# Postmix with the seventh block of keys once per set of rows, and the last batch's rows written ahead of its ranking

## The chip, the cores and the metric

The kernel runs on one core of one Trainium2 chip. The metric is the time of one execution in microseconds of device time; less is better.

## The reference

Three layers in a row, in float32. Batch 4, 12 heads, 448 tokens of 64 values per head; then 1792 tokens of 768 values.

```python
scores = scale * np.matmul(q, k.transpose(0, 1, 3, 2))
scores = np.einsum('bhij,hg->bgij', scores, w_pre)       # premix of heads
attn = softmax(scores)                                   # rows divided by their sum + 1e-9
attn = np.einsum('bhij,hg->bgij', attn, w_post)          # postmix of heads
x = np.matmul(attn, v)                                   # then heads side by side: 1792 x 768
h = x @ w_in                                             # 768 -> 2048
x = elu(h) @ w_out                                       # 2048 -> 768
logits = x @ w_gate                                      # 8 experts, the best one is taken
for e in range(8):
    mask = argmax(logits) == e
    out[mask] = gate_w[mask, None] * (np.maximum(x[mask] @ w1[e], 0) @ w2[e])
```

## The kernel before, in words

One program of three stages, each with its own pools of tiles.

**Attention** (`attention`, to about 393 us). 448 queries of a batch are cut in four chunks (120, 120, 120 and 88 tokens), 16 chunks in all. The scores of a chunk (`qk`, L221, tile p_qk) are copied out and laid out again by DMAs (`relayout`, L238), so that 12 heads x T tokens (T is 5, in one set per batch 4) stand on 60 partitions; that is a row, and a set holds nr = 2 of them in each of two halves c of the 128 partitions. There are 92 sets: 88 with two rows and T = 5, 4 with one row and T = 4. Per set: `premix` (L247, p_pre) multiplies by the 60x64 matrix kpre; `rowmax` and `expo` (DVE, ACT) give pt, 128 x 2 x 448; `scale` (L268) makes kp, the postmix matrix of 60 columns with each row's reciprocal sum in it; `postmix` (L281, p_post) takes 64 keys of pt as weights and kp as moving operand, so that its result has the keys on the partitions; `mt_out` (L291, ACT) copies that to mt. `av` (L316, p_av) then multiplies mt by the values vt, 128 keys at a time, three times for each chunk.

448 keys are seven blocks of 64. The result of postmix has four columns of 128 keys, so the last has room for 128 where 64 are left: the loop makes eight products for seven blocks, the eighth (`k0 = min(s, 6)`) a repetition of the seventh, and `values` sets the upper 64 rows of the last block of values to zero with a GpSimd memset (L183). All operands are float32, and each matmul of the program stands in the trace as two records. Postmix uses 64x64 tiles of the array: the row half is c, the column half is s % 2.

The order of the work is made by a planner: `at(slot, order, fn)` files each step under a slot of the stage, and the steps run by slot and then by order. SP's queue issues the loads, POOL's the relayouts.

**The dense layer** (`moe1`, to about 880 us). The last batch is computed last: `omm(f)` adds up 16 slices of the output projection into acc (L579); in the last slice `evac(d)` copies each of six blocks of 128 outputs to x2, and `wide` (L604) and `logits` (L608, with L590) make the gate's logits for them. `route(b, x2)` returns the list of routing steps of a batch. For the last batch, ahead of the experts, nothing else is left to run beside them: `pick` (DVE, the expert of each token), `row(t, hf)` (three transposes of tile tp, L90, a copy by ACT, L639, and with hf = 1 the DMA of 112 tokens' rows to memory, L642, tile x2rows), `rank` (L689 to L728, the token's place with its expert), `ship` (the gates' DMA, L646), `sort` (L736, L738), `warm` (20 matmuls whose result nobody reads, L816), `order` (`places` makes sel, then the experts' order; SP reads it into registers, L776), `deal([first])` (tok1, the first expert's tokens, L786 and L790), and `before_end[2]`, which gathers that expert's rows (`gather`, xg, L1150). The first expert's weights w1raw are loaded at an address that hangs on the order (L1126).

**The experts** (`moe2`, to the end). `prep` splits a weight into a high and a low part (w1h by ACT, L110; w1l by DVE, L112), `trans` transposes the gathered rows (p_t, L90), `run` multiplies (p_h, L1203).

Of the kernel before, what the change touches and what calls it, by code (L numbers as in the profile page):

```python
# [5 lines left out]
F32 = mybir.dt.float32  # L6
# [4 lines left out]
ALU = mybir.AluOpType  # L11
# [136 lines left out]
S0 = [0]  # L148
# [6 lines left out]
def attention(tc, pools, at, q, k, v, kron_pre, kron_post, dec_jobs, xscr):  # L155
# [14 lines left out]
    kpo = sb.tile([128, 1, 60], F32, name="kpo")  # L170
    nc.gpsimd.dma_start(kpo[:, 0], kron_post)
    dec = Decoder(nc, early, DM // 2, 2, 2, 2)

# [6 lines left out]
    def values(b):  # L180
        vt[b] = sb.tile([128, 4, H, D], F32, name="vt", tag="vt", bufs=2)

        nc.gpsimd.memset(vt[b][S - 384:, 3], 0.0)  # L183

# [76 lines left out]
    def scale(cc, g):  # L261
        T, nr = UNITS[cc % 4][g]
        sm = sms.pop((cc, g))[:, :nr]
        nc.vector.tensor_scalar(sm, sm, 1e-9, None, ALU.add)
        nc.vector.reciprocal(sm, sm)
        kp = kpt[cc, g] = sb.tile([128, 2, 60], F32, name="kp", tag="kp", bufs=3)
        sh = [128, nr, 60]
        nc.vector.tensor_tensor(kp[:, :nr], kpo.to_broadcast(sh), sm.unsqueeze(2).to_broadcast(sh), ALU.mult)  # L268

    def postmix(cc, g):  # L270
        T, nr = UNITS[cc % 4][g]
        e, kp = pt.pop((cc, g)), kpt.pop((cc, g))
        p = pst[cc, g] = post_bank()
        for j in range(4):
            for r in range(nr):
                for s in range(2 * j, 2 * j + 2):

                    k0 = min(s, 6)
                    for c in range(2):
                        x = slice(64 * c, 64 * c + 12 * T)  # L280
                        mm(p[64 * (s % 2):64 * (s % 2) + 64, 2 * c + r, j * 12 * T:(j + 1) * 12 * T],  # L281
                           lhsT=e[x, r, 64 * k0:64 * k0 + 64],
                           rhs=kp[x, r].rearrange("p (h i) -> p h i", i=5)[:, :, :T], start=True, stop=True)

# [8 lines left out]
    def load_v(b, j):  # L293
        if j == 0 and b:
            values(b)
        n = min(128, S - 128 * j)
        nc.sync.dma_start(vt[b][:n, j], v[b, 128 * j:128 * j + n])

# [112 lines left out]
def moe1(tc, pools, at, w_in, w_out, w_gate, consts, xscr, wscr, oscr, x2rows, R, before_end):  # L411
    nc = tc.nc
    mm = nc.tensor.matmul
    P, x2 = {}, {}
    xs, xraw, rows32, wi, wo, hp, gs, es, op, acc, cst = ({} for _ in range(11))
    last_b = NB - 1

# [154 lines left out]
    def omm(f):  # L572
        (wh, wl), (gh, gl) = wo.pop(f), gs.pop((f, last_b))
        for d in range(KD):
# [5 lines left out]
            if f == NF - 1:  # L580
                evac(d)
                if d >= 2:
                    wide(d - 2)
        if f == NF - 1:
            lg = P["sb"].tile([128, DM], F32, name="lg", tag="dec_p", bufs=3)[:, :S]
# [7 lines left out]
    def evac(d):  # L593
        if d == 0:
            x2[last_b] = P["x2"].tile([128, KD, S], F32, name="x2", tag="x2", bufs=NG)
        if d % 2 == 0:
            nc.scalar.activation(x2[last_b][:, d, :], acc[d][:, :S], AF.Copy)
        else:
            nc.vector.tensor_copy(x2[last_b][:, d, :], acc[d][:, :S])
# [10 lines left out]

    def route(b, x2):

        sb, base = P["r"], cst["base"]
        sh = [JC, NJ, NE]
        last = b == NB - 1
        T, banks = {}, [0]

# [10 lines left out]
        def row(t, hf):  # L628
            if hf == 0 and last:
                if t % 2 == 0:  # L630
                    T["rows"] = P["sb"].tile([128, 2 * DM], F32, name="rows", tag="raw", bufs=2)[:JC]
                T["row"] = T["rows"][:, t % 2 * DM:(t % 2 + 1) * DM]
            elif hf == 0:
                T["row"] = P["sb"].tile([128, DM], F32, name="row", tag="dec_p", bufs=3)[:JC]
            p = bank([JC, 3, 128], "tp")
            for i in range(3):
                transpose(nc, p[:, i, :], x2[:, 3 * hf + i, t * JC:(t + 1) * JC], cst["ident"])
            dst = T["row"][:, hf * 384:(hf + 1) * 384].rearrange("p (a c) -> p a c", a=3)
            nc.scalar.activation(dst, p, AF.Copy)  # L639
            if hf == 1:  # L640
                r0 = 1 + b * S + t * JC
                nc.sync.dma_start(x2rows[r0:r0 + JC, :DM], T["row"])  # L642

# [126 lines left out]
        def order():  # L770
            places()
            gt, key = T["gt"], T["key"]
# [37 lines left out]
        if last:  # L810
            first = PLACES[0]

            def warm():
                p, t = bank([128, 512], "warm"), xs[b, 0][0]
                for i in range(20):
                    mm(p[:, :S], lhsT=t[:, :128], rhs=t, start=True, stop=True)  # L816

            def others():
                deal(range(NE))
                targets()  # L820

            return [pick, *rows[:2], rank, *rows[2:4], ship, *rows[4:], sort, warm, order,
                     lambda: deal([first]), before_end[2], others, keep, over]
        return [wide, rows[0], lambda: (narrow(), pick()), *rows[1:3], rank, *rows[3:6], sort,
# [123 lines left out]
    def rest():  # L948
# [20 lines left out]

        steps, banks, late = [], [0], []  # L970
        for n in range(3, NU + 1):
# [68 lines left out]
        for f in range(NF + 1):  # L1040
            if f < NF:
                hmm(f, last_b, h_bank)
                if steps:
                    steps.pop(0)()
                elu((f, last_b))
            if f >= 1:
                omm(f - 1)
                if f == NF:
                    assert not steps
                    steps += route(last_b, x2[last_b])  # L1050
                elif steps:
# [381 lines left out]
```

## Time and profile before

| | us, or a count |
|---|---|
| three runs | 1212.44, 1217.86, 1216.82 |
| their median | 1216.82 |
| the profiled execution | 1212.38 |
| its span in the trace | 1210.6 |
| PE busy | 1150.7 (95%) |
| DVE, ACT, POOL busy | 766.8, 684.0, 297.0 |
| PE instructions of the page | 13498, of them postmix 5760 |

The page is of one execution. Busy times are sums over instructions, a PE record's end is modelled, and matmuls on different 64x64 tiles of the array run at once, so the records of a line overlap. What a step costs is therefore read from the chain of waits, where each piece starts when the one before it lets go.

### The profile page before, as it was taken

How to read it: one execution, taken by the hardware profiler on the slowest of the kernel's cores; microseconds unless marked ns; L12 is line 12 of the kernel's file. 1: busy time of each engine (PE TensorE's matmuls, PEld its weight loads, DVE VectorE, ACT ScalarE, POOL GpSimd, SP SyncE). 2: the span in 40 equal slices, each digit the busy share in tenths (PEclk: the TensorE clock that was granted, in tenths of full speed). 3: DMA queues.
4: the chain of work that ended last, by engine and by line, in shares of the span. 5: the costliest groups of instructions: out<-in, count | busy, mean ns of one | idle time of the engine just before them, and what ended most of it. 6: DMA issues, size and time to landing. Idle time of an engine off the chain costs nothing.

```text
span 1210.6 us, 32469 instructions
## 1 busy us (share of the span) xinstructions
PE 1150.7 (95%) x13498; PEld 977.0 (81%) x13498; DVE 766.8 (63%) x1537; ACT 684.0 (57%) x1310; POOL 297.0 (25%) x470
## 2 busy tenths in 40 slices
PE   5899999989998999999999998999989999999995
PEld 1566656656676999999999987989779999999995
DVE  3766867766765778677776656545455555656662
ACT  2877877767866665555556344555434444555552
POOL 4755656646640003011121100000010110111110
PEclk8999999999998999999999999999979999999998
DMA  7687798886664436556482723334165755666651
GB/s 210 182 227 183 185 232 201 206 210 167 169 185 127 145 112 173 153 128 159 111 222 69 182 68 98 107 122 139 40 208 202 240 168 175 202 241 221 205 197 62
DMA packets 115617, 200.76 MB, mean 166 GB/s; under 512 B 44896, under 2 KB 75346, under 8 KB 115460
## 3 DMA queue, kind: packets, MB, share of 16 engines
q1 hardware_dynamic: 77284, 137.22, 36.2%
q0 software_dynamic: 38176, 61.37, 20.8%
q8 instruction: 108, 1.77, 0.7%
q14 instruction: 49, 0.40, 0.1%
HBM read 120.15 MB, written 30.09 MB: 124 GB/s over the span
## 4 chain that ended last, share of the span: by engine, by line
PE 87%; ACT 4%; DMA 3%; DVE 3%; issue 2%; POOL 0%; SPq 0%; POOLq 0%; ACTq 0%; DVEq 0%
PE p_h L513 14%; PE p_o L553 14%; PE p_h L1203 12%; PE p_z L1188 8%; PE p_post L281 7%; PE p_av L316 7%; PE p_pre L247 6%; PE p_qk L221 5%; PE acc L579 5%; PE p_o L513 4%; PE p_y L1203 3%; DMA sp<-st 2%; PE p_t L90 1%; ACT mt L291 1%; PE tp L90 1%
## 5 line engine op out<-in xcount | busy, mean ns | idle before, releaser
L238 POOL DMA_DIRECT2D sp<-st x360 | 207.5, 595 | 138.4 <-PE p_pre L247 69.4
L258 ACT ACTIVATE pt<-p_pre,mx 128x448 f32<-128x448 f32 x180 | 112.6, 632 | 48.1 <-DVE mx L252 47.9
L281 PEld LDWEIGHTS p_post<-kp,pt 60*64 60x64 f32 (+1 forms) x5760 | 96.4, 135 | 49.4 <-ACT mt L291 30.9
L291 ACT ACTIVATE mt<-p_post 128x960 f32<-128x960 f32 (+1 forms) x92 | 101.6, 1104 | 38.0 <-PE p_post L281 38.0
L281 PE MATMUL p_post<-kp,pt 60*64 60x60 f32 (+1 forms) x5760 | 108.2, 220 | 14.6 <-issue 9.9
L252 DVE TENSOR_REDUCE mx<-p_pre 128x1 f32<-128x448 f32 x180 | 104.1, 618 | 28.3 <-PE p_pre L247 22.1
L570 POOL DMA_DIRECT2D x<-part x46 | 41.5, 926 | 295.1 <-ACT part L569 289.4
L1203 PE MATMUL p_h<-xgh,w1h 128*128 128x256 f32 (+1 forms) x384 | 110.3, 287 | 0.2 <-DVE h2l L1206 0.2
L1203 PE MATMUL p_h<-xgl,w1h 128*128 128x256 f32 (+1 forms) x384 | 110.0, 286 | 0.2 <-DVE xgl L1167 0.2
L1203 PE MATMUL p_h<-xgh,w1l 128*128 128x256 f32 (+1 forms) x384 | 109.9, 286 | 0.0
L553 PE MATMUL p_o<-gh,woh 128*128 128x448 f32 x288 | 106.5, 370 | 2.6 <-DVE x L566 2.6
L221 PE MATMUL p_qk<-ks,qs 64*64 64x448 f32 x744 | 96.9, 552 | 12.7 <-issue 4.7
L247 PE MATMUL p_pre<-sp,kpre 60*64 60x448 f32 x720 | 100.9, 550 | 5.4 <-DMA sp<-st 5.4
L553 PE MATMUL p_o<-gl,woh 128*128 128x448 f32 x288 | 105.2, 365 | 0.0
L553 PE MATMUL p_o<-gh,wol 128*128 128x448 f32 x288 | 104.9, 364 | 0.0
L316 PEld LDWEIGHTS p_av<-mt,vt 128*64 128x64 f32 x1536 | 76.6, 141 | 32.9 <-DVE kp L268 9.9
L228 DVE COPY st<-p_qk 128x448 f32<-128x448 f32 x93 | 57.8, 622 | 71.5 <-PE p_qk L221 64.0
L112 DVE TENSOR_TENSOR w2l<-w2raw,w2h 128x768 fp32r<-128x768 f32 (+1 forms) x60 | 60.7, 1012 | 51.4 <-ACT w2h L110 51.4
L533 DVE SCALAR_TENSOR_TENSOR th<-rm,th 128x448 f32<-128x448 f32 x64 | 40.0, 625 | 80.0 <-ACT rm L532 80.0
L316 PE MATMUL p_av<-mt,vt 128*64 128x120 f32 (+1 forms) x1536 | 86.4, 268 | 1.4 <-issue 0.9
L1239 POOL DMA_INDIRECT out_dram<-yrow,put x18 | 23.8, 1321 | 254.2 <-ACT w1h L110 86.9
L112 DVE TENSOR_TENSOR w1l<-w1raw,w1h 128x768 fp32r<-128x768 f32 x64 | 61.0, 960 | 28.5 <-ACT w1h L110 26.4
(196 smaller groups left out, 2800.7 us busy)
## 6 DMA issues: line engine op xcount, KB each, us to landing
sp<-st POOLq DMA_DIRECT2D x352, 105.0 KB
w1raw<-in_w_dram SPq DMA_DIRECT2D x64, 384.0 KB, 6.9
w2raw<-in_w_dram SPq DMA_DIRECT2D x48, 384.0 KB, 3.4
x<-part POOLq DMA_DIRECT2D x46, 224.0 KB
raw<-in_w_in_dram SPq DMA_DIRECT2D x13, 768.0 KB, 4.1
raw<-in_w_out_dram SPq DMA_DIRECT2D x13, 768.0 KB, 7.6
wtmp<-wscr SPq DMA_DIRECT2D x19, 384.0 KB, 3.5
wtmp<-oscr SPq DMA_DIRECT2D x19, 384.0 KB, 4.1
```

The lines of the kernel that those rows point to most:

```text
L112: nc.vector.tensor_tensor(l, src, a.bitcast(F32), ALU.subtract)
L221: mm(p[e][64 * a:64 * a + 64, :S], lhsT=qq[r, c:c + 64], rhs=kk[r], start=True, stop=True)
L238: nc.gpsimd.dma_start(t[64 * r:64 * r + 12 * T, c], st[cc][f:f + d * (T - 1) + 1:d])
L247: mm(ban[r][64 * c:64 * c + 64, :S], lhsT=kpre[x], rhs=t[x, c, :], start=True, stop=True)
L252: nc.vector.tensor_reduce(mxs[cc, g][:, r:r + 1], pre[cc, g][r][:, :S], AX.X, ALU.min)
L258: nc.scalar.activation(pt[cc, g][:, r], pre[cc, g][r][:, :S], AF.Exp, bias=mxs[cc, g][:, r:r + 1], scale=-1.0, accum_out=sms[cc, g][:, r:r ...
L281: mm(p[64 * (s % 2):64 * (s % 2) + 64, 2 * c + r, j * 12 * T:(j + 1) * 12 * T], lhsT=e[x, r, 64 * k0:64 * k0 + 64], rhs=kp[x, r].rearrange ...
L291: nc.scalar.activation(dst, src, AF.Copy)
L316: mm(p[64 * e:64 * e + 64, u, :n], lhsT=vt[cc // 4][:, j, h, :], rhs=mt[cc][:, j * H + h, :n], start=(j == 0), stop=(j == 3))
L513: mm(p[:, :S], lhsT=a[:, c], rhs=m, start=(i == 0), stop=(i == 17))
L553: mm(p[:, :S], lhsT=a[:, c], rhs=m, start=(k == 0), stop=(k == 3 * len(fs) - 1))
L1203: mm(q[:, :N], lhsT=a[:, kk, :], rhs=m[:, kk, :], start=(j == 0), stop=(j == len(seq) - 1))
```

## The change

In `postmix` six blocks are multiplied as before, in another order of the loops. The seventh is multiplied once for each row: the product of row r goes to the column half h = r, and its moving operand is two of three neighbouring 60-column parts of kp, of which the middle one holds zeros: kp[0:2] for h = 0 and kp[1:3] for h = 1. So the upper half of the result's last column belongs to row 1 and the lower to row 0, with zeros for the other row, and the values of the last 64 keys are loaded twice, into both halves. kp becomes three fixed tiles. In `moe1`, four of the last batch's eight half rows run in the last slice of `omm`, after the fourth, fifth and sixth block; the other four run ahead of `rank`; each half row has its own DMA. `places` runs ahead of `ship` and `sort`; the first expert's tokens and its gather run ahead of `order`. `warm` has 24 matmuls.

```diff
+    kps = [sb.tile([128, 3, 60], F32, name=f"kp{i}") for i in range(3)]
+    for kp in kps:
+        nc.vector.memset(kp[:, 1], 0.0)
...
-        nc.gpsimd.memset(vt[b][S - 384:, 3], 0.0)
...
-        kp = kpt[cc, g] = sb.tile([128, 2, 60], F32, name="kp", tag="kp", bufs=3)
+        kp = kpt[cc, g] = kps[(S0[cc] + g) % 3]
...
-        nc.vector.tensor_tensor(kp[:, :nr], kpo.to_broadcast(sh), sm.unsqueeze(2).to_broadcast(sh), ALU.mult)
+        nc.vector.tensor_tensor(kp[:, ::2][:, :nr], kpo.to_broadcast(sh), sm.unsqueeze(2).to_broadcast(sh), ALU.mult)
...
-        for j in range(4):
+
+        def prod(s, r, c, out, w):
+            x = slice(64 * c, 64 * c + 12 * T)
+            mm(out, lhsT=e[x, r, 64 * s:64 * s + 64],
+               rhs=kp[x, w].rearrange("p w (h i) -> p w h i", i=5)[:, :, :, :T], start=True, stop=True)
+
+        for s in range(6):
             for r in range(nr):
-                for s in range(2 * j, 2 * j + 2):
-
-                    k0 = min(s, 6)
-                    for c in range(2):
-                        x = slice(64 * c, 64 * c + 12 * T)
-                        mm(p[64 * (s % 2):64 * (s % 2) + 64, 2 * c + r, j * 12 * T:(j + 1) * 12 * T],
-                           lhsT=e[x, r, 64 * k0:64 * k0 + 64],
-                           rhs=kp[x, r].rearrange("p (h i) -> p h i", i=5)[:, :, :T], start=True, stop=True)
+                for c in range(2):
+                    h, j = slice(64 * (s % 2), 64 * (s % 2) + 64), s // 2 * 12 * T
+                    prod(s, r, c, p[h, 2 * c + r:2 * c + r + 1, j:j + 12 * T], slice(2 * r, 2 * r + 1))
+        for h in range(2):
+            for c in range(2):
+                prod(6, min(h, nr - 1), c, p[64 * h:64 * h + 64, 2 * c:2 * c + nr, 36 * T:48 * T], slice(h, h + nr))
...
         n = min(128, S - 128 * j)
-        nc.sync.dma_start(vt[b][:n, j], v[b, 128 * j:128 * j + n])
+        for o in range(0, 128, n):
+            nc.sync.dma_start(vt[b][o:o + n, j], v[b, 128 * j:128 * j + n])
...
                 if d >= 2:
                     wide(d - 2)
+                if d >= 3:
+                    for fn in at_end[:2 if d == KD - 2 else 1]:
+                        fn()
+                        at_end.remove(fn)
...
-        T, banks = {}, [0]
+        T, banks = {}, [-1]
...
-            if hf == 1:
-                r0 = 1 + b * S + t * JC
-                nc.sync.dma_start(x2rows[r0:r0 + JC, :DM], T["row"])
+            r0, c0 = 1 + b * S + t * JC, hf * 384 if last else 0
+            if hf == 1 or last:
+                nc.sync.dma_start(x2rows[r0:r0 + JC, c0:(hf + 1) * 384], T["row"][:, c0:(hf + 1) * 384])
...
         def order():
-            places()
...
-                for i in range(20):
+                for i in range(24):
...
-            return [pick, *rows[:2], rank, *rows[2:4], ship, *rows[4:], sort, warm, order,
-                     lambda: deal([first]), before_end[2], others, keep, over]
+            at_end.extend(rows[::2])
+            rows = rows[1::2]
+            return [pick, *rows, rank, places, ship, sort, warm,
+                     lambda: deal([first]), before_end[2], order, others, keep, over]
```

The instructions of TensorE in the attention stage, a set's premix (p_pre), postmix (p_post) and the queries' products (p_qk) that follow. Before:

```order
L247 MATMUL p_pre_568<-sp_353,kpre_119 64x448
L247 MATMUL p_pre_569<-sp_353,kpre_119 64x448
L247 MATMUL p_pre_568<-sp_353,kpre_119 64x448
L247 MATMUL p_pre_569<-sp_353,kpre_119 64x448
L281 MATMUL p_post_588<-kp_576,pt_516 64x60 x32
L221 MATMUL p_qk_629<-ks_130,qs_290 64x448
L221 MATMUL p_qk_630<-ks_130,qs_290 64x448
```

Now, at a like place:

```order
L248 MATMUL p_pre_493<-sp_290,kpre_119 64x448
L248 MATMUL p_pre_494<-sp_290,kpre_119 64x448
L278 MATMUL p_post_512<-kp0_124,pt_441 64x60 x24
L278 MATMUL p_post_512<-kp0_124,pt_441 64x2x60 x4
L222 MATMUL p_qk_548<-ks_135,qs_295 64x448
L222 MATMUL p_qk_549<-ks_135,qs_295 64x448
```

32 products of 60 columns became 24 of 60 and 4 of twice 60; what stands around them stayed.

TensorE at the end of the dense layer: wide logits (p_h of 32 rows), the narrow ones (p_h of 112 x 8), the transposes of rows (tp of 112 x 128) and the ranking's products (rp). Before:

```order
L604 MATMUL p_h<-x_11745,wg 32x448
L608 MATMUL p_h<-wg,x_11745 112x8 x4
L590 MATMUL p_h<-sel,lg 112x8 x4
L608 MATMUL p_h<-wg,x_11745 112x8 x4
L90 MATMUL tp<-c_ident,x_11745 112x128 x6
L689 MATMUL rp<-base,c_ones 128x8
L690 MATMUL rp<-r_tot,c_tri 112x8
L691 MATMUL rp<-r_tot,c_ones 128x8
L90 MATMUL tp<-c_ident,x_11745 112x128 x18
L736 MATMUL tp<-tab,c_ident 128x24
```

Now:

```order
L615 MATMUL p_h<-x_11307,wg 32x448
L90 MATMUL tp<-c_ident,x_11307 112x128 x3
L619 MATMUL p_h<-wg,x_11307 112x8 x4
L601 MATMUL p_h<-sel,lg 112x8 x4
L619 MATMUL p_h<-wg,x_11307 112x8 x4
L90 MATMUL tp<-c_ident,x_11307 112x128 x12
L701 MATMUL rp<-base,c_ones 128x8
L702 MATMUL rp<-r_tot,c_tri 112x8
L703 MATMUL rp<-r_tot,c_ones 128x8
L748 MATMUL tp<-tab,c_ident 128x24
```

Three of the twelve early transposes show here, nine stand further ahead between the last slice's products; the other twelve are now in front of the ranking, where six were, and none is behind it.

VectorE at the end of routing: the places (r_pos, r_sel), the order of the experts, the first expert's tokens (tok_102) and all tokens (128 x 192). Before:

```order
L766 TENSOR_REDUCE r_pos<-r_gt 128x8
L768 SCALAR_TENSOR_TENSOR r_sel<-r_pos,c_em_6836 128x64
L773 TENSOR_TENSOR r_gt<-r_sel,c_em_6836 1x64
L774 TENSOR_REDUCE r_key<-r_gt 1x8
L775 TENSOR_SCALAR order<-r_key 1x8
L786 TENSOR_TENSOR pick<-tp,r_sel 128x24
L790 TENSOR_REDUCE tok_102<-pick 128x3
L786 TENSOR_TENSOR pick<-tp,r_sel 128x192
```

Now:

```order
L778 TENSOR_REDUCE r_pos<-r_gt 128x8
L780 SCALAR_TENSOR_TENSOR r_sel<-r_pos,c_em_6423 128x64
L797 TENSOR_TENSOR pick<-tp,r_sel 128x24
L801 TENSOR_REDUCE tok_102<-pick 128x3
L784 TENSOR_TENSOR r_gt<-r_sel,c_em_6423 1x64
L785 TENSOR_REDUCE r_key<-r_gt 1x8
L786 TENSOR_SCALAR order<-r_key 1x8
L797 TENSOR_TENSOR pick<-tp,r_sel 128x192
```

The three operations of the order moved behind the two that make the first expert's tokens. On SP's queue the last batch's transfers were two rows, the gates, two rows, and then the read of the order; they are now eight half rows, the gates, and the read of the order.

## Rows read from the trace of the kernel before

**Rows 1.** Part 1 of the page: engine, busy us, share, instructions.
```profile
PE 1150.7 (95%) x13498; PEld 977.0 (81%) x13498; DVE 766.8 (63%) x1537; ACT 684.0 (57%) x1310; POOL 297.0 (25%) x470
```

**Rows 2.** Part 4 of the page: shares of the chain by engine.
```profile
PE 87%; ACT 4%; DMA 3%; DVE 3%; issue 2%; POOL 0%; SPq 0%; POOLq 0%; ACTq 0%; DVEq 0%
```

**Rows 3.** Windows, attention: PE, PEld, DVE, ACT, POOL, clock, DMA share, GB/s.
```profile
20.00:380.00 360.00, 332.83 (x8650) 221.87 (x8651) 249.75 (x667) 263.72 (x566) 204.91 (x355) 0.99 0.74 191
```

**Rows 4.** Chain in order of time, attention: start, us, what, records.
```profile
199.68 0.45 PE p_post L281 x32
...
202.26 1.79 PE p_av L316 x32
...
206.65 1.36 PE p_av L316 x32
...
210.62 0.93 PE p_post L281 x64
```

**Rows 5.** Timeline of PE at the first postmix: start, us, what.
```profile
30.62 0.60 PE L247 MATMUL p_pre<-sp,kpre 60*64 60x448 f32 x3
30.99 0.26 PE L281 MATMUL p_post<-kp,pt 60*64 60x60 f32 x1
31.05 0.55 PE L247 MATMUL p_pre<-sp,kpre 60*64 60x448 f32 x3
```

**Rows 6.** Waits of PE, 24 to 380: total us, times, longest.
```profile
PE p_post L281 <- issue: 9.9, 11, 1.9
PE p_pre L247 <- DMA sp<-st: 5.4, 1, 5.4
PE p_qk L221 <- issue: 4.7, 3, 3.2
```

**Rows 7.** Part 3 of the page, instruction queue: packets, MB, share.
```profile
q8 instruction: 108, 1.77, 0.7%
```

**Rows 8.** Line 183: times, ns min/median/max, first and last start.
```profile
L183 POOL MEMSET vt<- x4: 732/777/787, 2.6 to 259.3; 64x768 f32 x4
```

**Rows 9.** Chain in order of time, at 839 and between the stages.
```profile
839.22 0.33 PE tp L90 x3
...
879.93 0.80 PE p_h L608 x8
...
882.13 0.54 PE rp L690 x2
...
883.10 3.93 PE tp L90 x18
...
887.58 3.30 DMA x2rows<-rows
...
891.76 1.06 POOL xg L1150
...
893.13 4.50 DMA xg<-x2rows,tok
...
897.67 1.54 PE p_t L90 x6
899.21 0.93 PE p_h L1203 x4
```

**Rows 10.** Timeline of ACT between the stages, idle time in brackets.
```profile
881.34 0.85 ACT L639 ACTIVATE rows<-tp 112x384 f32<-112x384 f32 x2
883.86 3.69 ACT L639 ACTIVATE rows<-tp 112x384 f32<-112x384 f32 x6 [1.67 <-PE tp L90]
```

**Rows 11.** Timeline of DVE between the stages.
```profile
887.63 0.18 DVE L790 TENSOR_REDUCE tok<-pick 128x3 uint32<-128x24 f32 x1
...
893.84 0.96 DVE L112 TENSOR_TENSOR w1l<-w1raw,w1h 128x768 fp32r<-128x768 f32 x1 [3.52 <-ACT w1h L110]
```

**Rows 12.** Timeline of SP between the stages.
```profile
889.21 10.01 SPq L1126 DMA_DIRECT2D w1raw<-in_w_dram  x7
```

**Rows 13.** Windows, the start of the experts; columns as in rows 3.
```profile
896.00:902.00 6.00, 5.72 (x26) 5.32 (x27) 2.93 (x7) 3.40 (x10) 1.26 (x2) 0.50 0.89 287
```

More of the change, by code (lines that the diff above doesn't have):

```diff
@@ L415, in moe1 @@
     xs, xraw, rows32, wi, wo, hp, gs, es, op, acc, cst = ({} for _ in range(11))
+    at_end = []
     last_b = NB - 1
@@ L594, in evac @@
         if d == 0:
-            x2[last_b] = P["x2"].tile([128, KD, S], F32, name="x2", tag="x2", bufs=NG)
+            x2[last_b] = P["x2_last"] = P["x2"].tile([128, KD, S], F32, name="x2", tag="x2", bufs=NG)
         if d % 2 == 0:
@@ L609, in logits, with route @@
                start=(d == KD - 2 and t == 0), stop=(d == KD - 1 and t == NJ - 1))
-    def route(b, x2):
+    def route(b, x2=None):
         sb, base = P["r"], cst["base"]
@@ L628, in row @@
         def row(t, hf):
[L629 to L632, printed above, removed]
+            if last:
+                if (t % 2, hf) == (0, 0):
+                    T["rows", t // 2] = P["sb"].tile([128, 2 * DM], F32, name="rows", tag="raw", bufs=2)[:JC]
+                T["row"] = T["rows", t // 2][:, t % 2 * DM:(t % 2 + 1) * DM]
             elif hf == 0:
@@ L635, in row @@
             p = bank([JC, 3, 128], "tp")
+            y = P["x2_last"] if last else x2
             for i in range(3):
-                transpose(nc, p[:, i, :], x2[:, 3 * hf + i, t * JC:(t + 1) * JC], cst["ident"])
+                transpose(nc, p[:, i, :], y[:, 3 * hf + i, t * JC:(t + 1) * JC], cst["ident"])
             dst = T["row"][:, hf * 384:(hf + 1) * 384].rearrange("p (a c) -> p a c", a=3)
             nc.scalar.activation(dst, p, AF.Copy)
-            if hf == 1:
-                r0 = 1 + b * S + t * JC
-                nc.sync.dma_start(x2rows[r0:r0 + JC, :DM], T["row"])
+            r0, c0 = 1 + b * S + t * JC, hf * 384 if last else 0
+            if hf == 1 or last:
+                nc.sync.dma_start(x2rows[r0:r0 + JC, c0:(hf + 1) * 384], T["row"][:, c0:(hf + 1) * 384])
         def ship():
@@ L968, in weights @@
             load_pair(f + 3)
-        steps, banks, late = [], [0], []
+        steps, banks, late, last_steps = [], [0], [], []
         for n in range(3, NU + 1):
@@ L1045, in rest @@
                 elu((f, last_b))
+            if f == NF:
+                last_steps += route(last_b)
             if f >= 1:
@@ L1049, in rest @@
                     assert not steps
-                    steps += route(last_b, x2[last_b])
+                    steps += last_steps
                 elif steps:
```

## The prediction

> **What bounds the kernel now.** I read the share of busy time first: TensorE is busy for 95% of the span [rows 1]. That is an average over three stages, so the chain of waits comes next: 87% of it is TensorE [rows 2]. The change touches two places. The first is the attention stage, from 20 to 380 us: there TensorE is busy 333 of 360 us, ScalarE 264, VectorE 250, GpSimd 205 [rows 3]. A time saved on TensorE shortens this stage, and no other engine is near to becoming its bound. The second is the step from the dense layer to the experts, between 880 and 899 us, where the chain leaves TensorE for VectorE, ScalarE and DMAs [rows 9].
>
> What does a postmix cost? Follow the pieces of the chain one by one [rows 4]. A set with 60 moving columns is 64 records in 0.93 us. They go to four 64x64 tiles of the array that work at once, so each tile makes 16 passes, and a round of four passes takes 0.93/16 = 58 ns. The set of 48 columns has 8 rounds in 0.45 us, 56 ns. A fifth fewer columns save 2 ns: at this width a pass is not set by its columns but by what comes with every pass, its weights. Value products (p_av) of 120 and 88 columns take 1.79/16 = 112 and 1.36/16 = 85 ns a round, so there 32 columns cost 27 ns, 0.84 ns each. By that slope 60 columns alone would be 50 ns, under the 58 measured, and a round of 120 columns about 50 more, 101; the p_av row itself says at most 112. I take 103.
>
> Do the tiles wait for each other? The timeline of the first postmix answers [rows 5]. One tile starts its postmix at 30.99; the other three tiles start their second premix passes only at about 31.05 and run them for 0.55 us. So a tile whose operands are there starts ahead of the others, and the order of the program counts only through how far it lies ahead in the queue.
>
> What the stage loses besides is in the waits [rows 6]: 9.9 + 4.7 = 14.6 us of "issue", when nothing visible holds TensorE up, and once 5.4 us for the first relayout. Instructions come from memory in packets, 108 in the whole run [rows 7].
>
> **Postmix, the product.** 88 of 92 sets have two sets of rows. Per set the change takes 8 products of 60 columns away (the seventh block, twice for each of two row sets and two column halves) and puts 4 of 120 columns in their place: 32 products become 28, the moving columns stay at 1920. Per tile 16 rounds of 58 ns become 12 of 58 and 2 of 103: 928 ns become 902, about -27 ns. The four sets of 48 columns keep their 16 products; zeros add columns to four of them, under 0.1 us each, which I cost at nothing.
>
> The order of the tiles changes too. Before, four products in a row go to four tiles; now two row sets follow each other on the same two tiles, and only then come the other two tiles. The second pair starts later by about one round, 58 ns; the bounds are nothing and two rounds, 117 ns. The query and premix products that follow start tile by tile, as in [rows 5], so the lag stays on its tiles and does not grow. It is paid where the next product needs both halves of the rows at once: that is p_av, three for each of 16 chunks, 48 in all. So 88 sets save 27 ns (-2.4 us) and 48 times a lag of 58 is paid (+2.8). I take **+0.4 us**; the bounds are -2.4 us (no lag) and 90 x 88 = +7.9 us (two rounds in every set).
>
> **Postmix, the instructions.** Each of the 88 sets loses 8 product records and 8 weight loads: 1408 of the stage's 17,301 [rows 3], 8.1%. If the issue stalls are instruction packets that come late, they shrink in proportion: 8.1% of 14.6 is **-1.2 us**. Between nothing and half of them (-7.3 us) I have no row that decides; it is the proportion that the count gives.
>
> **kp and the values.** VectorE writes the same 120 elements into every other column, and three fixed tiles are cleared at the start, while TensorE has no work; nothing. The GpSimd clearing of values goes: 4 x 0.78 us [rows 8] on an engine busy for 205 of 360 us, hidden before and worth nothing now. In its place 64 keys' values are loaded twice, four DMAs of 64 x 768 x 4 = 197 KB more on SP's queue: at 191 GB/s [rows 3] 1.0 us each. Three lie far from any need. The first, at the start, can push back the relayout for which TensorE waits 5.4 us; **+0.3 us**, between 0 and 1.0.
>
> **The step to the experts.** Call the end of the logits lp; before, 879.93 + 0.80 = 880.73 [rows 9]. Twelve transposes move ahead of it: at 0.33/3 = 0.11 us each, +1.32 us. ScalarE has the copy that follows one of them in front of the logits' own copy: 0.85/2 = 0.43 us [rows 10]. So lp comes 1.75 us later.
>
> Before, 18 transposes came after the ranking's products in 3.93 us, 0.218 each, twice the 0.11, and the last row transfer took 3.30 and landed at 890.88, lp + 10.15; the gather was built from 891.76 [rows 9]. Now 12 transposes in four pieces are left: the first piece 3 x 0.218 = 0.65, then four copies at 3.69/6 = 0.61 [rows 10], then 3.30: lp + 6.4. The gather also needs the tokens, at 887.63 + 0.18, lp + 7.08 [rows 11]. Three VectorE operations of the order (0.65 us with their gaps) and a wait of 0.26 for TensorE no longer stand in front: lp + 6.2. But the ranking's products now queue behind 12 transposes, lp + 1.3 at full clock, lp + 2.6 at half, where it was lp + 1.40 [rows 9]: up to 1.2 later, so lp + 6.2 to 7.4. The gather is free at lp + 6.4 to 7.4 in place of 10.15: -2.7 to -3.7 against +1.75. I take **-1.5 us** net.
>
> Two things are late next. The first expert's weight load cannot go before the order is read: it was issued at 889.21, lp + 8.48 [rows 12]; the order is now made behind the tokens, so about 0.4 to 0.6 later against lp. Its splitting ended at 893.84 + 0.96 [rows 11], 5.6 us after the issue, so now near lp + 14.6; the first product, at 899.21 before [rows 9], would start at lp + 18.5 - 3.2 = lp + 15.3: just hidden. It takes up to 1 us if the gather gains all. And the clock: TensorE goes from 896 to 902 at half its clock, 0.50, the 1.2 GHz level [rows 13], after TensorE had waited for the gather's 4.50 us [rows 9]. Four more warming products and a shorter gap may spare part of this; at most half of the 1.54 us of transposes and 0.93 of first products [rows 9], -1.2. I take nothing. Bounds of this step: -3.2 and +0.5. SP has eight row transfers instead of two pairs, each half as long and issued as soon as its copy is done; that is in the path above, and the gate's transfer stays last.
>
> **Sum.** 0.4 - 1.2 + 0.3 - 1.5 = -2.0 us against the profiled execution, 1212.4 us, so 1210.4. That execution is the fastest of four: the median of the runs is 1216.8 and the mean of all four 1214.9. Against that mean a new median would be **1212.9 us**. A difference under 0.5% (6.1 us) can hardly be told from none here, so "same" is 1210.7 to 1222.9.
>
> **Rivals.**
> *Fetching was the limit (0.20).* If the stalls come from a fetch that is only just too slow, 8% fewer instructions can take half of them: -7.3 instead of -1.2, 1206.8 us. For it: 14.6 us without a visible cause. Against it: they are 14 stalls of up to 3 us, not a steady shortfall.
>
> *Tiles in program order (0.09), the slower side.* If a product had to wait for the one before it, whichever its tile, the new order would make each pair a step of its own: two products of 117 ns on the same tiles before the other pair moves, 7 x 117 + 206 = 1025 ns per set and up to 58 more, against 928. Then +97 to +155 ns x 88 = +8.5 to +13.6, in the middle +11.1 instead of +0.4: 1223.6 us. It decides from about 118 ns per set on (118 x 88 = 10.4, which ends at 1222.9). Against it: one tile starts alone [rows 5]. The Trainium skill ("TensorE: Matmul & The Clock Gate", Part 3, "The mechanism") says that matmuls start and end strictly in the order of the program; by that rule this rival would hold. What hangs on it here is only whether a start at 30.99 ahead of one at 31.05 was in program order.
>
> *Loads and products take turns (0.03).* If, in a tile, a weight load could not run under the product before it, every load removed would save its full length: two passes fewer per tile, 2 x 58 = 116 ns x 88 = -10.2 us in place of +0.4, 1202.3 us. Against it: 16 passes of 58 + 50 = 108 ns would take 1.73 us and the row says 0.93 [rows 4]. The Trainium skill (same page and section) says that weight loads overlap running matmuls only when the row groups differ, which would be this case for passes of one tile; the measured 58 ns a round disagree.
>
> *The step gains nothing (0.08).* The ranking or the weight load takes the place of the rows: 1214.4 us.
>
> **Chances.** The forecast has 0.60; of it 0.10 falls under 1210.7 and 0.02 over 1222.9, since the runs shown spread over 5 us. Faster: 0.10 + 0.20 + 0.03 = 0.33. Slower: 0.09 + 0.02 = 0.11. Same: 0.56. The range, 1205.0 to 1221.5, takes in the fetch rival at its low end and, at its high end, the bound of two late rounds (1212.9 + 7.5 = 1220.4, and 1.1 of the other bounds); it leaves out the program-order and the take-turns rivals, 0.12, and the forecast's tails.
>
> **What would show it.** Postmix pieces of the chain near 0.90 us; 1.02 or more everywhere means program order. Issue waits of about 13.4 us in the stage. The row transfers landed and the gather issued about 2 us earlier, near 889 to 890, and the first expert product near 897.7. I am wrong if attention as a whole moves by more than 5 us either way.

## The result, and the profile after

The change ran at a median of 1203.55 us (1198.01 to 1206.79, six runs), the kernel before in the six runs beside it at 1215.95 (1212.44 to 1220.33): 12.4 us less. The ratio of the two is 0.9869 with an interval of 0.9837 to 0.9901; the quotient of these two medians, 0.9898, lies inside it. Forecast were 1212.9 us and a range of 1205.0 to 1221.5: the gain is real, larger than forecast, and ends under the range. The profiled execution took 1198.01 us, the fastest of its six; that of before, 1212.38 us, was faster than all six of before. They are 14.4 us apart.

Where the 14.4 us lie, by the starts and ends of TensorE's records in the two traces:

| stretch | before | change | difference |
|---|---|---|---|
| start to first postmix | 31.0 | 32.2 | +1.2 |
| first to last postmix | 347.7 | 336.2 | -11.5 |
| last postmix to the end of the last acc | 498.7 | 499.0 | +0.3 |
| end of the last acc to the first expert product | 21.5 | 18.1 | -3.4 |
| first expert product to the end | 311.7 | 310.7 | -1.0 |

Four fifths are in the attention stage. Part 1 of the page after, part 3's row of the instruction queue and part 4, to be held against [rows 1, 7, 2]:

```profile
PE 1148.1 (96%) x12798; PEld 975.4 (82%) x12798; DVE 766.2 (64%) x1540; ACT 683.5 (57%) x1310; POOL 295.4 (25%) x466
...
q8 instruction: 103, 1.69, 0.6%
...
PE 88%; ACT 4%; DVE 3%; DMA 2%; issue 1%; POOL 0%; SPq 0%; POOLq 0%; ACTq 0%; DVEq 0%
```

TensorE is busy 2.6 us less, the span is 14.4 us shorter: what went is mostly time in which TensorE stood still. 700 matmuls and five packets of instructions are gone. The waits of TensorE in the attention stage after, against [rows 6]; columns: total us, times, longest:

```profile
PE p_post L278 <- issue: 4.9, 6, 1.5
PE p_post L278 <- ACT mt L296: 4.8, 8, 1.2
PE p_qk L222 <- ACT st L231: 2.8, 3, 1.0
...
PE p_pre L248 <- DMA sp<-st: 1.1, 1, 1.1
```

The issue waits (idle time of TensorE that nothing visible ends), 9.9 + 4.7 + 0.9 (ahead of p_av) = 15.5 us before, are 4.9. That is 10.6 of the stage's 11.5 us. One more piece goes with the longest of these stalls before. Timeline and windows there (columns as in [rows 3]):

```profile
269.64 0.59 PE L221 MATMUL p_qk<-ks,qs 64*64 64x448 f32 x2 [3.20 <-issue]
...
270.90:274.30 3.40, 3.40 (x30) 2.65 (x29) 2.57 (x8) 1.34 (x4) 1.93 (x4) 0.50 0.41 132
```

After 3.2 us of standing still the granted clock was 0.50, the 1.2 GHz level, for 3.4 us. Between the first and the last postmix of the change it was 1.00 throughout. The step to the experts in the chain of waits after, against [rows 9]:

```profile
870.67 0.80 PE p_h L619 x8
...
877.55 0.18 DVE tok L801
...
878.68 1.07 POOL xg L1165
879.75 0.30 issue
880.05 4.54 DMA xg<-x2rows,tok
884.64 0.34 PE p_t L90
```

The logits end at 871.47, the tokens stand at 877.73, 6.3 us later, and the gather is built from 878.68, 7.2 us after them, where before it was built 11.0 us after the logits. The row transfers are gone from the chain: the tokens are now what the gather waits for. The clock there, windows of the same trace (columns as in [rows 13]):

```profile
877.00:880.00 3.00, 3.00 (x10) 2.69 (x9) 2.58 (x15) 0.00 (x0) 1.07 (x1) 0.50 0.00 0
880.00:884.00 4.00, 3.59 (x21) 3.04 (x19) 1.30 (x5) 0.85 (x1) 1.01 (x1) 1.00 0.86 292
884.60:890.60 6.00, 5.55 (x41) 4.94 (x42) 4.24 (x9) 3.84 (x12) 2.73 (x3) 1.00 0.94 338
```

The first six us of the experts, at 0.50 before, ran at 1.00; the fall to 0.50 now comes earlier, and the first warming products ran in it (877 to 880).

### The profile page after: what moved, and what is told of

The parts are those of the page before. It is cut to its first block, busy times and chain, and to the rows that moved or that the text cites. A ratio compares the mean times of both kernels' runs of the same rounds, so it can differ in the third digit from the quotient of the medians.

```text
span 1196.2 us, 31070 instructions
## 1 busy us (share of the span) xinstructions
PE 1148.1 (96%) x12798; PEld 975.4 (82%) x12798; DVE 766.2 (64%) x1540; ACT 683.5 (57%) x1310; POOL 295.4 (25%) x466
## 4 chain that ended last, share of the span: by engine, by line
PE 88%; ACT 4%; DVE 3%; DMA 2%; issue 1%; POOL 0%; SPq 0%; POOLq 0%; ACTq 0%; DVEq 0%
PE p_h L520 14%; PE p_o L560 14%; PE p_h L1218 11%; PE p_z L1203 8%; PE p_post L278 7%; PE p_av L322 7%; PE p_pre L248 6%; PE p_qk L222 5%; PE acc L586 5%; PE p_o L520 4%; PE p_y L1218 3%; DMA sp<-st 1%; ACT mt L296 1%; PE p_t L90 1%; PE tp L90 1%
## 5 line engine op out<-in xcount | busy, mean ns | idle before, releaser
L278 PEld LDWEIGHTS p_post<-kp,pt 60*64 60x64 f32 (+1 forms) x5056 | 88.6, 134 | 44.1 <-ACT mt L296 31.1
L278 PE MATMUL p_post<-kp,pt 60*64 60x60 f32 (+2 forms) x5056 | 108.9, 228 | 10.0 <-issue 4.9
L248 PE MATMUL p_pre<-sp,kpre 60*64 60x448 f32 x720 | 105.9, 551 | 3.8 <-DMA sp<-st 3.8
L222 PE MATMUL p_qk<-ks,qs 64*64 64x448 f32 x744 | 100.0, 557 | 9.0 <-ACT st L231 5.1
L112 DVE TENSOR_TENSOR w1l<-w1raw,w1h 128x768 fp32r<-128x768 f32 x64 | 60.9, 960 | 28.3 <-ACT w1h L110 25.1
```

What stands on the lines that cost most here:

```text
L112: nc.vector.tensor_tensor(l, src, a.bitcast(F32), ALU.subtract)
L222: mm(p[e][64 * a:64 * a + 64, :S], lhsT=qq[r, c:c + 64], rhs=kk[r], start=True, stop=True)
L248: mm(ban[r][64 * c:64 * c + 64, :S], lhsT=kpre[x], rhs=t[x, c, :], start=True, stop=True)
L278: mm(out, lhsT=e[x, r, 64 * s:64 * s + 64], rhs=kp[x, w].rearrange("p w (h i) -> p w h i", i=5)[:, :, :, :T], start=True, stop=True)
```

## The experiments

The question was what took the issue waits away, since the forecast had given them 1.2 us. The theory: they are instruction packets that land late (a packet lands when its transfer is complete). The rivals: shorter products, the number of instructions, the burst within a set. Time ratios are to the kernel before on the same chip.

**The step alone, and postmix alone.** The first has the attention of before in the change, the second the `moe1` of before.

```diff
 # e1: attention() of before, moe1() of the change
 # e8: attention() of the change, moe1() of before
```

> The change without its attention part: only the step to the experts is as in the change. Both theories of the attention gain (late instruction packets; shorter products) expect the same here: the attention stage as before, issue waits of TensorE between 20 and 380 us near 15.5 us, the last postmix near 378.7 us. The step itself should give back what the two traces differ by behind the last slice of the dense layer, -3.2 us: about -3 us against before, and the wait for the gather to end about 13.2 us after the logits instead of 16.9.

> The attention part of the change alone, with the old step to the experts. If the parts add up: the ratio to before that is left of the change's 0.987 without the step's 0.998 (2.8 us by the traces), 0.989, so 11 to 13 us under before; issue waits of 5 to 9 us. If the step carried more than the step-alone run could show: 8 us or less.

Measured: the step alone 0.9994 (0.9966 to 1.0023), issue waits 9.5 + 4.2 + 1.5 = 15.2 us. Postmix alone 0.9922 (0.9891 to 0.9953), 9.5 us less; its issue waits, forecast at 5 to 9 us, are 12.3 in the profiled execution, the slowest of its eleven (1215.78 us). So most of the gain is postmix's. The step is too small for the runs; in the traces, the stretch from the last postmix to the end takes 829.1 us on average (827.4 to 830.2) in nine executions of this study that have it (e16, with 828.4, not counted), and 831.1 (829.7 to 832.5) in the six that don't, 2.0 us less. 9.5 and 2.0 are 11.5, near the 12.4 of the medians (16.3 by e13's medians).

**30 products, 32 products, another order of tiles.**

```diff
 # e2, on before
+                    if s == 7 and r:
+                        continue
+                    n = nr if s == 7 else 1
...
-                        mm(p[64 * (s % 2):64 * (s % 2) + 64, 2 * c + r, j * 12 * T:(j + 1) * 12 * T],
+                        mm(p[64 * (s % 2):64 * (s % 2) + 64, 2 * c + r:2 * c + r + n, j * 12 * T:(j + 1) * 12 * T],
...
-                           rhs=kp[x, r].rearrange("p (h i) -> p h i", i=5)[:, :, :T], start=True, stop=True)
+                           rhs=kp[x, r:r + n].rearrange("p w (h i) -> p w h i", i=5)[:, :, :, :T], start=True, stop=True)
 # e3, on the change
-                prod(6, min(h, nr - 1), c, p[64 * h:64 * h + 64, 2 * c:2 * c + nr, 36 * T:48 * T], slice(h, h + nr))
+                for i in range(nr):
+                    prod(6, min(h, nr - 1), c, p[64 * h:64 * h + 64, 2 * c + i:2 * c + i + 1, 36 * T:48 * T],
+                         slice(h + i, h + i + 1))
 # e4, on the change
-        for s in range(6):
+        for s2 in range(3):
             for r in range(nr):
-                for c in range(2):
+                for s, c in ((2 * s2, 0), (2 * s2, 1), (2 * s2 + 1, 0), (2 * s2 + 1, 1)):
 # e7: e4 with e3's products, i as the outer loop
```

> The kernel before, in which the repeated eighth product is made once for each half of the rows, with 120 moving columns, instead of twice with 60 (what it gives is multiplied by the zeros in the values, as before). 30 products for a set instead of 32, half of the change's cut in instructions, and the tiles of the other column half keep their 16 passes, so that a set takes as long as before. If late instruction packets were the limit: issue waits well under 15.5 us, between 5 and 12, and the time 3 to 8 us under before. If the products had become shorter: nothing is gained, within 1 us of before, and the issue waits stay near 15 us.

> The change, with each of its four products of 120 columns cut into two of 60: 32 products for a set again, and all else as in the change. If late instruction packets were the limit: issue waits back at 13 to 17 us, while a set that nothing interrupts is at most 30 ns longer than in the change; the time 8 to 13 us over the change, about that of the step alone. If the weight loads that are saved were the gain, undisturbed sets become longer by 60 to 120 ns each and the issue waits stay near 5 us. If neither, the time is within 3 us of the change.

> The change, with its 24 products of 60 columns in the old order, in which four products in a row go to four tiles. By the prediction's lag of one round, paid at each of 48 value products, this gains 2.8 us and the pieces ahead of value products get shorter by some 58 ns; if the lag is not paid, the time is within 1 us of the change. If tiles in program order cost anything, it gains 8 us or more.

> The rotating version of the change with its four products of 120 columns cut into eight of 60 that go round the four tiles: 32 products, the order of before, the step to the experts as in the change. It differs from the rotating version by 4 products a set and nothing else. Late packets: issue waits at 14 to 16 us again, and 9 to 13 us over the change, about 1216; the undisturbed set as long as before. If the 14.8 us that the unpaired version lost were all due to its order of tiles: within 3 us of the change.

Measured: 30 products 0.9954 (0.9929 to 0.9979), issue waits 13.5 us, where 5 to 12 were expected; 32 products in the new order 1.0006 (0.9979 to 1.0033), 15.0 us; 28 products in the old order of tiles 0.9877 (0.9840 to 0.9913), 9.2 us; 32 products in the old order 1.0045 (1.0013 to 1.0076). The waits of the third, e4, and of the last, e7, which differ in the number of products alone:

```profile
PE p_post L278 <- issue: 7.1, 7, 2.2
...
PE p_qk L222 <- issue: 1.4, 1, 1.4
...
PE p_av L322 <- issue: 0.7, 1, 0.7
```

```profile
PE p_post L278 <- issue: 10.5, 13, 2.2
...
PE p_qk L222 <- issue: 4.2, 3, 2.9
...
PE p_av L324 <- issue: 1.6, 2, 1.2
```

Four products a set, 8% of the instructions, bring the issue waits back to 16 us. The order of the tiles is worth nothing (1204.86 against 1203.55 us): the lag of one round that the forecast charged at p_av is not paid. In the five traces with 32 products in one piece and all loads (before, e1, e3, e7, e11) the issue waits are 15.0 to 16.3 us; in the six with 28 (the change, e4, e8, e12, e13, e14) 4.9 to 12.3. The ranges do not overlap.

The rival of shorter products has a part. Take the sets without value products that nothing interrupts for over 100 ns, at full clock, from the first product of a set to that of the next. The median is 2491 ns in before, e1, e7 and e15 (32 products), 2478 in e2 (30) and 2464 in the change, e4, e8, e13 and e14 (28), over 35 to 45 sets in each. 27 ns for each of 88 sets are 2.4 us at most. With the 7.3 us by which the issue waits fell on average (below) that comes near e8's 9.5.

e7 is the slowest of these, 1224.13 us, though e1 with as many products is level with before. In the traces its attention stage is 5.9 us longer than e1's, 1.1 of it issue waits; in e7 the clock was at 0.50 for three stretches of 3.4 us between first and last postmix, in e1 for none.

**Burst within a set.** A set's products in two halves, with the query products between (e5 on before, e6 on the change), or with p_av between (e10 on before).

```diff
-            at(x + LAG + .5, 10, postmix, cc, g)
+            at(x + LAG + .5, 10, postmix, cc, g, 0)
+            at(x + LAG + 1, 9.5, postmix, cc, g, 1)
...
 # e10: slots x + LAG + .5 with orders 8.5 and 10
```

> The kernel before, with each set's 32 products in two halves of 16 and the next query products (8 records in 0.76 us) between them: as many instructions as before, but no more than 64 product records in a row. If the stalls come from the burst, that is, a packet is used up within a set faster than the next one comes: issue waits well under 15.5 us, 3 to 9, and 5 to 10 us less time. If they go by the number of instructions alone: issue waits stay at 14 to 16 us and the time within 2 us of before. The copy of a set to mt comes 0.8 us later; where TensorE waits for that copy, 4.6 us in all before, it may wait up to 4 us more.

> The change with its 28 products split in the same way, 16 and then 8 and 4 of 120 columns. If the burst makes the stalls: the 5 to 9 us of issue waits that the change and its rotating version still have fall under 3, and the time is 3 to 6 us under the change. If the number makes them: no change, within 2 us.

> The kernel before, with a set's 32 products in two halves of 16 around the value products (p_av) where a set has them: 48 of 92 sets have no more than 64 product records in a row, the order of all else and the waits for ScalarE stay. Two forms of the theory of late packets are told apart, since the split around the query products was mixed up with 21 us of new waits for ScalarE. If the burst within a set makes the stalls: issue waits fall from 15 to about 8 us and the time by 5 to 8 us. If it is the pace over a whole packet of 256 instructions (some 4 us, more than a set): nothing changes, issue waits 13 to 17 us and the time within 3 us of before.

Measured: 1.0045 (1.0016 to 1.0074), 0.9974 (0.9951 to 0.9996), 1.0108 (1.0072 to 1.0143). All lost against what they were made from. Waits of e6:

```profile
PE p_post L280 <- ACT mt L298: 20.9, 42, 1.2
...
PE p_qk L222 <- issue: 0.5, 1, 0.5
PE p_post L280 <- issue: 0.5, 1, 0.5
```

The issue waits fell (8.0, 1.2 and 6.7 us), but p_post has one buffer in PSUM, and its next products wait for ScalarE's copy: 21.8, 20.9 and 18.9 us. So these runs say nothing on the burst by itself: they slowed the stage, and a slower stage needs its packets later.

**Pace.** The value products in halves, one in each of two sets; and the change once more beside them.

```diff
...
-        half(y, 9, av, cc, a)
+        if soon:
+            half(y, 9, av, cc, a)
+        else:
+            half(y, 9, av, cc, a, (0,))
+            half(y + 2, 9, av, cc, a, (1,))
+            y += 1
```

> The kernel before, in which the value products of a chunk go in halves, 8 in each of two sets instead of 16 in every other set. The same instructions, the same sets; only the pace is more even: a set without p_av has 160 instructions in 0.93 + 0.76 + 0.75 = 2.44 us (256 in 3.9 us), with half a p_av 192 in about 3.35 us (256 in 4.5 us); the change without p_av has 144, 256 in 4.3 us. Pace over a packet: issue waits fall from 15 to 2 to 8 us and the time by 6 to 12 us, with not one instruction less. Number of instructions: no change, within 2 us. Burst within a set: no change either.

> The change with the same halves: 176 instructions in about 3.35 us, 256 in 4.9 us. Pace over a packet: the 5 to 10 us of issue waits that the change still has fall under 3 us, and the time is 3 to 7 us under the change run beside it, 1196 to 1201 us. Number or burst: within 2 us of the change.

> The change itself, on the same chip as the three beside it: 11 to 16 us under before, a ratio of 0.987 to 0.991; issue waits of 5 to 9 us in one more execution.

Measured: 1.0004 (0.9972 to 1.0035) and 0.9956 (0.9926 to 0.9986); the change 0.9873 (0.9829 to 0.9916), 1203.25 us. My expectation failed: an even pace won nothing. Each half p_av costs 0.97 us in the chain where a whole one costs 1.79, so some 0.15 us more for each pair, and the issue waits did not fall, 15.7 us in e11; in e12 they are 12.3, more than in the change.

**What the packets do.** In the records of the 15 issue stalls of before, the 6 of the change, the 11 of e13 and the 14 of e1, TensorE (matmuls, weight loads and its semaphore instructions, counted from the first, which is number 0) always goes on with number 193 modulo 256, and does so 1.2 to 1.7 us after a packet of the instruction queue (16,384 bytes each) has landed. So a packet is 256 instructions, TensorE had used up the last one, and every one of these stalls is a late packet. Over all 17 traces it is 182 of 183 stalls, 1.2 to 2.1 us after a landing. That gives two numbers for each packet between 40 and 355 us: how long its 256 instructions last (from the start of the first to that of the last) and when the next lands, from the same start.

```text
kernel                packets  last: median, shortest   under 3.7 us: number, stall   others: stall   next lands (mean)
before (32 products)     62      4.73   3.14               12   10.3 us                 4.5 us          2.82
e1 (32)                  63      4.75   3.14               12   10.6                    4.6             2.79
e2 (30)                  60      4.86   3.24                6    3.5                   10.0             3.02
change (28)              60      5.33   3.67                3    0.3                    4.6             2.98
e13, the change (28)     60      5.34   3.68                2    0.0                    6.6             2.97
e8 (28)                  57      5.34   3.68                2    0.0                   12.3             3.11
e11 (32, halves)         61      4.40   3.40                1    0.4                   15.3             3.16
e15 (32, fewer loads)    63      4.74   3.09               11    2.7                    6.7             2.56
```

In the kernel before a fifth of the packets lasts under 3.7 us (a bound chosen after the fact, near the change's shortest), and two thirds of the stall time stands behind these. The change has hardly any left: what it keeps, 4.6 to 12.3 us, stands behind packets of ordinary length that the next one followed late. In e8 the landing came 5.0 us after the first instruction, on average, where TensorE stalled, against 3.1 over all packets. The landing differs between executions and kernels: e11 has one short packet, but they land 0.34 us later.

An estimate from before's own packets shows why the stalls fall by more than the instructions do. Take for a stall what is left of landing + 1.45 us - length, and give every packet 0.5 us more, as much as the change's last longer on average (5.2 us against 4.7): the sum falls from 20.0 to 11.7 us, by 42%. The sums are above the measured 14.8 us; only their ratio is used.

**DMA load.** Less in the kernel before, more in the change.

```diff
 # e15, on before; queries and values likewise
         if b:
-            keys(b, u)
+            ks[b, u] = ks[0, u]
+            return
 # e16, on the change, in relayout; extra is a tile that nobody reads
+        nc.sync.dma_start(extra[:48], v[cc // 4, :48])
```

> The kernel before without the loads of the queries, keys and values of the last three batches: the first batch's tiles are used again (left out: the attention of batches 2 to 4 on their own data), so that some 12 of 69 MB that the stage moves are gone and TensorE's instructions, their order and all other work stay. In the trace of before a packet lands on average 2.8 us after TensorE has entered the 256 instructions ahead, with a spread of 1.0, and these last 4.8 us, the shortest 3.2. If the stalls are the overlap of these two spreads and the transfers delay the packets: landing near 2.4 us, issue waits between 4 and 10 us instead of 15, the time 5 to 11 us under before. If the number of instructions alone makes them: issue waits at 13 to 17 us, within 2 us of before.

> The change with a load of 147 KB from memory for each of the 92 sets, which nobody reads (13.6 MB more in the stage). Overlap of spreads: packets land later, 3.2 us and more on average instead of 3.0, issue waits from 5 to 9 up to 12 or more, the time 4 to 10 us over the change. Number alone: issue waits of 5 to 9 us, within 2 us of the change.

e15's total (1506 us) can't be read: its routing is that of other data and needs a further pass (14,314 matmuls against 13,498). Its attention stage can. The window from 20 to 380 us, against [rows 3], and its waits:

```profile
20.00:380.00 360.00, 339.26 (x8740) 227.10 (x8734) 253.87 (x674) 269.12 (x576) 202.42 (x350) 0.98 0.57 157
```

```profile
PE p_post L285 <- issue: 9.4, 9, 2.9
```

DMA share 0.57 instead of 0.74, packets land after 2.56 us, 9.4 us of issue waits with the same instructions in the same order, and first to last postmix 342.6 us instead of 347.7. So the load of the DMA engines looks like a second part of the cause. This is one trace: 9.4 us is well under the 15.0 to 16.3 of the other traces with 32 products in that pace, but packets land after 2.58 us in e5 as well, with all its loads and longer sets. e16 failed as an experiment: each extra load waited on SP's queue for the one before, and what stood behind them came late (p_post waited 28.5 us for kp, p_qk 8.4 for queries; 1.0438). Its 16.4 us of issue waits can't be told apart from that.

**The clock.**

```diff
-                for i in range(24):
+                for i in range(20):
```

> The change with 20 warming products instead of 24. If the four more kept TensorE's clock up until the gather: the granted clock of the first 6 us of the experts falls back to 0.50, the first products take twice as long and the experts' stage starts 1 to 1.5 us later against the end of the dense layer. If the earlier gather alone did it: clock 1.00 there as in the change, and no difference.

Two runs, ratio 0.9879 (0.9815 to 0.9942). The windows:

```profile
888.00:890.00 2.00, 0.88 (x6) 0.64 (x6) 0.96 (x1) 0.84 (x1) 0.00 (x0) 1.00 0.70 226
890.00:896.00 6.00, 5.41 (x38) 4.69 (x39) 4.33 (x9) 4.51 (x12) 2.76 (x3) 1.00 0.97 308
```

With 20 warming products the clock is 1.00 as well. TensorE stood still for 1.3 us ahead of the first gathered rows here, for 0.4 in the change, for 3.7 before, where the clock fell. In all ten traces with the new step TensorE stood still for 0.4 to 1.3 us there and ran the next six us at 1.00; in the seven with the old step it stood still for 3.7 to 5.2 us and ran them at 0.50 to 0.68. So the earlier gather keeps the clock, and the four more products are not needed for it.

## Why the prediction was wrong, point by point

- **The bound was right.** The time came out of TensorE's path in attention, and no other engine became the bound.
- **The step that failed is "8.1% of 14.6 is -1.2 us".** The forecast knew the packets and guessed that stalls shrink in proportion to the instructions. They shrank from 15.5 and 15.2 us (before, e1) to 4.9, 6.6, 8.4 and 12.3 in four executions of the change's attention (the change, e13, e14, e8), on average by 7.3 us. So the forecast's own sign of being wrong, attention moving by more than 5 us, came: -11.5. A stall is the little that a landing is later than 256 instructions last, so it does not shrink in proportion: two thirds of before's stall time stood behind its shortest packets, and these are gone, while stalls behind the latest landings stayed. The rival "fetching was the limit", -7.3 us, is nearest to what happened, and it had 0.20. That the mean is 7.3 as well is luck: half was a guess, and the four executions lie between -3 and -10. That a few rows showed 14 separate stalls was taken against this rival, where it was its mark.
- **The product's length: half right.** The 27 ns for each set were right, 2491 ns before and 2464 after. The lag of +2.8 us was not paid: e4, without it, is no faster. So this term is up to -2.4 us where +0.4 was forecast. First to last postmix is 341.2 us on average in those four and 347.3 in before and e1, -6.1 us; without the issue waits that is +1.2, but the clock is in it. At 0.50 it cost time in before (one stretch of 3.4 us), e13 (one), e14 (two) and e8 (10.2 us); TensorE's busy time there is 322.4 us in the change and 323.9, 325.9 and 327.0 in e13, e14 and e8, some 1.5 us for each 3.4. Four of the six stretches came with or just after an issue stall of 2.3 to 3.2 us. The forecast had no term for this in attention. Without any such stretch the change's 322.4 us stand against e1's 323.8.
- **Program order of tiles did not happen.** It would have made each set over 90 ns longer. The Trainium skill's rule ("TensorE: Matmul & The Clock Gate", Part 3, "The mechanism") would give that; no run here agrees with it, since an undisturbed set takes 2464 ns in either order.
- **Loads and products in turns did not happen either:** two passes fewer per tile shortened a set by 27 ns, not by 116.
- **The step to the experts: right.** Logits 1.75 us later was forecast; from the first acc products of the last slice to the logits' end the chain takes 11.91 us after and 10.27 before, 1.64 more. The tokens were forecast at lp + 6.2 to 7.4, measured 6.3. The transposes ran near full clock (12 in 1.50 us), so the ranking was not held up. In e13, the same kernel, the clock was at 0.50 from 873.0 to 876.4, they took 2.79 us and the tokens came at lp + 7.0: both ends of the forecast occur. The experts began at 1.00, for which nothing was taken. In the pair of traces the rest of the program is 4.1 us shorter, on average of fifteen executions 2.0; -1.5 was forecast.
- **The start** moved by +1.2 us here, but first postmixes began between 30.0 and 33.4 us whatever the kernel did with the values (e2 30.0, e8 33.4). On average that is 31.9 us in nine traces with values loaded twice and 31.0 in six without; with a scatter of 1.0 in each a cost is not shown, and one of up to 1 us, the forecast's bound, is not excluded. Only e15, without the later batches' loads (25.1), and e16 (29.2) began earlier.

Still open is what sets the landing: why it is 2.8 us in one kernel and 3.2 in another of the same traffic was not tried apart from the loads. It is also open why four executions of the same attention differ by 7 us in their stalls, and why a long stall was not always followed by the lower clock (e1 stood still for 2.9 us and kept 1.00). The ratio (0.9869, 16 us) is larger than the parts (11.5); postmix's own interval, 6 to 13 us, leaves room for most of it. No version that was run beats the change.

## What to carry to other kernels

An idle time of TensorE without a releaser is worth a count: if its records, semaphore instructions included, stop at the same place of every 256, it is waiting for its instructions, and then small matmuls cost more than their time. Price a cut in instructions packet by packet, by how long each lasts against when the next lands: a stall is a difference between two times, and such differences don't shrink in proportion. Compare more than one trace of a kernel, since here the same kernel stalled for 4.9 and for 6.6 us, and look at the clock behind each long stall before a difference is put down to a product's length. Splitting work to spread the instructions costs more than it gives where a buffer is single.

## What was not expected of the hardware

Every one of 46 issue stalls in four traces stood at instruction 193 modulo 256 and ended 1.2 to 1.7 us after a 16 KB packet of the instruction queue landed. In the table's kernels packets landed 2.6 to 3.2 us, on average, after the 256 instructions ahead were begun (at most 7.3, in e8), while 256 instructions of postmix, premix and query products lasted as little as 3.1 us. In one execution with the DMA share at 0.57 instead of 0.74 they landed 0.26 us earlier, and the stalls were 9.4 us instead of 15.5. A stall can cost twice: 3.2 us of it in before were followed by 3.4 us at a granted clock of 0.50.
